# Attention and a gated feed-forward on one core: the value steps and the feed-forward of a batch start one score burst later, and v is normed ahead of the out copies

## The chip, the cores and the metric

The kernel runs on one core of one Trainium2 chip. A core has five engines that each work through their own queue in order: TensorE (PE in the profile) for matrix products, VectorE (DVE), ScalarE (ACT), GpSimd (POOL) and SyncE (SP), which here only issues DMA transfers. They wait for one another by semaphores. TensorE writes its products into PSUM, eight banks of 128 partitions x 2 KB; the other engines read them from there.

The metric is the time of one execution on the device in microseconds (us), as the median of several runs.

## The reference

The input is q (8 batches, 16 heads, 384 rows, 64 columns), k and v (8, 4, 384, 64), and the weights of a feed-forward layer. Each of the four k and v heads serves four q heads.

```python
scores = scale * np.matmul(q, k.transpose(0, 1, 3, 2))
attn = np.exp(scores - max) / sum            # softmax over the keys
x = np.matmul(attn, v)                       # heads side by side: 384 x 1024 per batch
h = np.maximum(x @ w_in, 0.0)                # 384 x 1024
u, v = h[..., :512], h[..., 512:]
v_n = (v - mean(v)) / np.sqrt(var(v) + 1e-06)
v_s = np.einsum('ts,bsd->btd', w_spatial, v_n) + b_spatial[None, :, None]
out = (u * v_s) @ w_out                      # 384 x 1024 per batch
```

## The kernel before

**Steps and a written order.** Every piece of work is a small step with a short name, and the order of the steps is written out by hand as text. `play` (L618) reads the words one after the other and calls the function behind each; the instructions reach each engine's queue in that order. A word without a mark belongs to batch b of the round, one with `'` to batch b-1, with `''` to b-2, with `+` to b+1. A round therefore works on four batches at once: attention scores of b, values and the middle of the feed-forward of b-1, the output product of b-2, loads for b+1.

**The steps**, with the engine that does them:

- `s` (L301): one score tile for two heads, two matmuls of 512 columns that run side by side in the two halves of the array's rows, into a pair of PSUM banks. `e` (L318): ScalarE's exp of that pair into aT, 1.02 us. A batch has 18 of them, s0 to s8 for the first group of heads and s9 to s17 for the second. They are played in bursts of three.
- `a` (L339): VectorE adds two of three key tiles of aT into sT (fp16). Six of them a batch (a00 to a02, a10 to a12).
- `m` (L352): TensorE sums aT over the keys with a matrix of ones. `r` (L359): ScalarE makes 1/sum by Ln and Exp. `x` (L374): values, attn times v. `n` (L387): VectorE multiplies the value tile by 1/sum into xT. The constants `C0` and `C1` (L638, L639) hold the sums, recs, values and norms of the first and of the second group of heads.
- `V` (L431): v half of x @ w_in for one third of the rows, and VectorE's relu from PSUM (L436). `S` (L443): mean and variance (L449, L450). `rs` (L452): ScalarE's 1/sqrt of the variance. `vn` (L457): VectorE norms v, three instructions (L460).
- `p` (L470): spatial product of one 128-column tile, and VectorE's bias add (L480). `U` (L484): u half, and VectorE's relu times v_s into gT (L493).
- `O` (L498): output product of half a row third, VectorE's copy to osb (L513), and after each second one the transfer to memory on the SP queue (L521). `Oc` is the same, done in four column groups of 32; `Oa` is the same with the copy on ScalarE.
- `lk lq lv` (L178 to L210): loads on the SP queue. `ck cq cv`: casts to fp16 on GpSimd (L189, L232, L200). `tk tq` (L249, L255): transposing transfers on the SP queue.

**PSUM banks.** `take1` and `take2` (L87 to L98) give out the bank, or the even pair of banks, that has been unused longest. A step that takes a bank waits for the last reader of what was in it. In a round the last burst behind V2, O2, O3 takes the two banks of V2 and O2, so it waits for VectorE's copy of O2; p0 and U0 take the banks of the values x010 and x011, so they wait for VectorE's norms.

**The round.** The list `VISITS` (L640) has six entries, each a burst of three score tiles and a block of other work. The first rounds (`RAMP`, `RAMP1`, `FIRST`) and the tail (`LAST`) have texts of their own. The loop that plays them stands at L667 to L671. In the steady text TensorE runs around a ring: burst, Oc pair and values of the second heads, burst, V0 V1, burst, V2 O2 O3, burst, Oc pair and values of the first heads, burst, p0 U0 p1 U1, burst, p2 U2 p3 U3, and again.

Of the kernel before, what the change touches and what calls it, by code (L numbers as in the profile page):

```python
# [13 lines left out]
ALU = mybir.AluOpType  # L14
# [3 lines left out]
def kernel(  # L18
# [11 lines left out]
    nc = tc.nc  # L30
# [145 lines left out]
    T = {}  # L176
# [159 lines left out]
                    stop=(t == n - 1),  # L336
                )

    def add(b, gp, c):  # L339
        aT = T["aT", b, gp]  # L340
        if ("sT", b, gp) not in T:
            T["sT", b, gp] = ff.tile([P, 2, G * S], FP16, name=f"sT_{b}_{gp}", tag="part")
        cs = slice(c * 512, (c + 1) * 512)
        nc.vector.tensor_tensor(T["sT", b, gp][:, :, cs], aT[:, 0, :, cs], aT[:, 1, :, cs], ALU.add)  # L344

    def add2(b, gp, c):
        T["all", b, gp] = True
        cs = slice(c * 512, (c + 1) * 512)
        sT = T["sT", b, gp][:, :, cs]
        nc.vector.tensor_tensor(sT, sT, T["aT", b, gp][:, 2, :, cs], ALU.add)  # L350

    def sums(b, gp, quad):  # L352
        x = take_of_pair(("sums", b, gp)) if b else take1()
# [103 lines left out]
    def v_norm(b, engine):  # L457
        for st in range(NST):
            v_n = vp.tile([P, DH], FP16, name=f"v_n_{b}_{st}", tag="v_n")
            engine.tensor_scalar(  # L460
                v_n,
                T["v_r", b, st],
                T["mv", b][:, st, 0:1],
                T["rstd", b][:, st : st + 1],
                op0=ALU.subtract,
                op1=ALU.mult,
            )
            T["v_n", b, st] = v_n
# [88 lines left out]
    def project_last(b, i, parts=2):  # L557
# [20 lines left out]


    STEPS = {  # L580
        "w": idle, "s": score, "e": expo, "m": sums, "a": add, "f": add2, "r": recip, "rd": recip_v, "x": value, "n": norm,
        "V": gate_v, "S": stats, "rs": rstd, "vn": lambda b: v_norm(b, nc.vector),
        "p": spatial, "U": gate_u, "O": project, "A": v_half, "H": u_half,
        "lk": load_k, "lq": load_q, "lv": load_v,
# [33 lines left out]
    def play(b, text):  # L618
        for word in text.split():
            kind = word.rstrip("'+")  # L620
            at = b - word.count("'") + word.count("+")
            op = kind.rstrip("0123456789")
            nums = kind[len(op):]
            if 0 <= at < B:
                STEPS[op](at, *([int(nums)] if op in ("s", "e", "w") else map(int, nums)))
# [12 lines left out]
    C1 = "m10' m11' r10' r11' x100' n100' x101' n101' x110' n110' x111' n111'"  # L638
    C0 = "m00 m01 r00 r01 x000 n000 x001 n001 x010 n010 x011 n011"  # L639
    VISITS = [  # L640
        "s0 s1 s2 e0 e1 e2 a12' Oc0'' Oc1'' lk+ lq0+ lv+ lq1+", C1,
        "s3 s4 s5 e3 e4 e5 V0' S0' V1' S1' a00 a01 ck+ cq0+",
        "s6 s7 s8 e6 e7 e8 V2' S2' O2'' O3'' tk+ tq0+ cq1+ cv+",
        "s9 s10 s11 e9 rs' e10 e11 a02 Oc4'' Oc5'' vn' tq1+", C0,
        "s12 s13 s14 e12 e13 e14 p0' U0' p1' U1' a10",
        "s15 s16 s17 e15 e16 e17 p2' U2' p3' U3' a11",
    ]
    STEADY = " ".join(VISITS)
    FIRST = """lk+ lq0+ lv+ lq1+
        s3 e3 s4 e4 V0' S0' s5 e5 V1' S1' ck+ cq0+  # L650
        s6 e6 s7 e7 V2' S2' s8 e8 Q11 tk+ tq0+ cq1+ cv+
# [1 line left out]
        s12 e12 s13 e13 p0' U0' s14 e14 p1' U1'   # L653
        s15 s16 s17 e15 e16 e17 p2' U2' p3' U3' a10 a11"""
    LAST = """
        a12' Oc0'' Oc1'' m10' m11' r10' r11' x100' n100' x101' n101' x110' n110' x111' n111'
        V0' S0' V1' S1' V2' S2' O2'' O3'' rs' vn' O4'' O5''
        pz0' pz1' pz2' pz3' Uz0' Uz1' O0' O1' Uz2' Oh2' Oh3' Oh4' Oz5'"""

    with tc.manual_schedule():  # L660
        play(0, RAMP)
        nc.vector.memset(warm, 0.0)
        make_identity(nc, ident)
        nc.vector.tensor_copy(ident16, ident)
        nc.vector.memset(ones32, 1.0)
        nc.vector.memset(eps_t, eps_ln)
        play(0, RAMP1)  # L667
        play(1, FIRST)
        for b in range(2, B):
            play(b, STEADY)  # L670
        play(B, LAST)  # L671
# [1 line left out]
_INS = ['q', 'k', 'v', 'moe_w_in', 'moe_w_spatial', 'moe_b_spatial', 'moe_w_out']  # L673
# [26 lines left out]
```

The softmax here doesn't subtract the row's maximum and nothing guards it: scores larger than these inputs give would overflow.

## Time and profile before

| what | us |
|---|---|
| median of 6 runs (256.51 to 259.99) | 257.25 |
| the profiled execution | 256.91 |
| its span, first to last instruction | 255.1 |
| TensorE busy in it | 240.2 |
| VectorE busy | 186.3 |
| ScalarE busy | 172.2 |
| GpSimd busy | 58.6 |
| one steady round, first V0 matmul of batch 5 to that of batch 6 (144.32 to 173.21) | 28.89 |

All times in the text are microseconds from the start of the profiled span, or lengths. The span is what the instructions cover; the execution has some 1.8 us around it. TensorE's granted clock was 0.996 over the span. Because the matmuls overlap, TensorE's time for a step is best read from the start of its first matmul to the start of the next step's.

### The profile page before, as it was taken

Reading aid. Unit: us, or ns where it says so; the run is one execution under the profiler, and the core shown is the slowest. Engines: PE = TensorE matmul, PEld = TensorE weight load, DVE = VectorE, ACT = ScalarE, POOL = GpSimd, SP = SyncE. Lnnn points to the kernel's source line nnn. Section 1 sums busy time; section 2 is a strip of 40 time slices with the busy share of each in tenths; the row PEclk is TensorE's granted clock in tenths of the full one; section 3 lists DMA queues with packets and bytes.
Section 4 is the critical chain, followed back from the end, with each engine's and each line's share of the span. In section 5 each row is a group of like instructions: output and inputs, shape, how many; then the busy total and the mean of one; then the engine's idle time right before and its main releaser. Section 6 shows DMA issues by size and latency. Waiting matters only on the chain.

```text
span 255.1 us, 6119 instructions
## 1 busy us (share of the span) xinstructions
PE 240.2 (94%) x2545; PEld 116.8 (46%) x2545; DVE 186.3 (73%) x348; ACT 172.2 (68%) x228; POOL 58.6 (23%) x100
## 2 busy tenths in 40 slices
PE   6689998999999999999999999999999999999993
PEld 5242434444444535553354434553454534554671
DVE  1534589997977599677977599577986599587953
ACT  3899799877767868677766958776776959730000
POOL 2627922604400064003700063001800000000000
PEclk9999999999999999999999999999999999999998
DMA  6999999959690779529591687519791204010424
GB/s 179 276 250 322 176 175 263 236 136 311 178 217 0 223 231 169 152 83 283 177 221 18 198 256 204 117 45 270 224 216 23 85 0 167 3 72 13 164 84 166
DMA packets 57228, 41.98 MB, mean 165 GB/s; under 512 B 26352, under 2 KB 53360, under 8 KB 57200
## 3 DMA queue, kind: packets, MB, share of 16 engines
q1 hardware_dynamic: 54208, 38.31, 55.8%
q0 software_dynamic: 2848, 3.15, 7.9%
q8 instruction: 20, 0.33, 0.5%
q10 hardware_dynamic: 144, 0.13, 0.1%
q14 instruction: 8, 0.07, 0.1%
HBM read 25.95 MB, written 12.58 MB: 151 GB/s over the span
## 4 chain that ended last, share of the span: by engine, by line
PE 58%; DVE 19%; DMA 11%; POOL 5%; issue 3%; SPq 2%; ACT 0%
PE banks L119 44%; DMA q<-in_q_dram 9%; PE banks L331 7%; PE banks L309 7%; DVE osb L513 3%; DVE sT L344 3%; DVE bn L449 3%; DVE v_n L460 3%; DVE v_r L436 3%; DVE xT L391 3%; DMA qT<-q 2%; POOL w_in L142 2%; POOL q L232 1%; SPq L183 1%; POOL ws L162 1%
## 5 line engine op out<-in xcount | busy, mean ns | idle before, releaser
L321 ACT ACTIVATE aT<-banks 128x1024 f16<-128x1024 f32 x144 | 137.5, 1024 | 48.6 <-PE banks L309 47.7
L309 PE MATMUL banks<-qT,kT 64*128 64x512 f16 x288 | 45.7, 380 | 6.6 <-DVE osb L513 2.0
L119 PE MATMUL banks<-xT,w_in 128*128 128x384 f16 (+1 forms) x320 | 47.2, 294 | 0.6 <-DVE v_r L438 0.6
L119 PE MATMUL banks<-w_out,gT 128*32 128x512 f16 (+2 forms) x508 | 45.4, 378 | 0.0
L119 PE MATMUL banks<-w_in,xT 128*128 128x512 f16 x192 | 44.7, 380 | 0.0
L391 DVE TENSOR_TENSOR xT<-banks,rec 128x384 f16<-128x384 f32 x64 | 31.4, 550 | 10.1 <-ACT rec L364 8.3
L232 POOL CAST q<-q 128x384 f16<-128x384 f32 x56 | 31.9, 602 | 17.2 <-DMA q<-in_q_dram 16.6
L119 PEld LDWEIGHTS <-w_in 128*128 128x128 f16 x320 | 27.2, 98 | 15.9 <-issue 1.4
L331 PE MATMUL banks<-aT,v 128*32 128x384 f16 x768 | 34.4, 326 | 0.0
L513 DVE COPY osb<-banks 128x512 f32<-128x512 f32 x47 | 31.4, 686 | 3.9 <-PE banks L119 3.8
L119 PEld LDWEIGHTS <-gT 128*32 128x32 f16 (+1 forms) x508 | 18.8, 96 | 27.9 <-issue 9.6
L189 POOL CAST k<-k 128x768 f16<-128x768 f32 x7 | 5.8, 830 | 102.3 <-DMA k<-in_k_dram 93.5
L119 PEld LDWEIGHTS <-xT 128*128 128x128 f16 x192 | 17.2, 98 | 25.6 <-issue 7.4
L344 DVE TENSOR_TENSOR sT<-aT 128x1024 f16<-128x1024 f16 x39 | 27.9, 744 | 0.0
L493 DVE SCALAR_TENSOR_TENSOR gT<-banks,vs 128x384 f16<-128x384 f32 x24 | 13.4, 558 | 17.0 <-PE banks L119 17.0
L331 PEld LDWEIGHTS <-v 128*32 128x32 f16 x768 | 20.4, 97 | 11.1 <-issue 0.9
L309 PEld LDWEIGHTS <-kT 64*128 64x128 f16 x288 | 11.3, 94 | 29.2 <-issue 22.8
L436 DVE TENSOR_SCALAR v_r<-banks 128x512 f32<-128x512 f32 x21 | 14.4, 688 | 11.8 <-PE banks L119 11.1
L119 PE MATMUL banks<-wsT,v_n 128*128 128x384 f16 x96 | 20.8, 327 | 0.8
L362 ACT ACTIVATE rec<-banks 128x384 f32<-128x384 f32 x32 | 15.7, 489 | 4.7 <-PE banks L331 4.3
L480 DVE TENSOR_TENSOR vs<-banks,bias_tp 128x384 f32<-128x384 f32 x28 | 15.6, 557 | 2.9 <-PE banks L119 2.9
L364 ACT ACTIVATE rec<-rec 128x384 f32<-128x384 f32 x32 | 16.7, 523 | 1.0
(49 smaller groups left out, 139.2 us busy)
## 6 DMA issues: line engine op xcount, KB each, us to landing
q<-in_q_dram SPq DMA_DIRECT2D x31, 384.0 KB, 7.0
out_dram<-osb SPq DMA_DIRECT2D x22, 512.0 KB, 3.2
v<-in_v_dram SPq DMA_DIRECT2D x8, 384.0 KB, 6.9
k<-in_k_dram SPq DMA_DIRECT2D x7, 384.0 KB, 5.2
w_in<-in_moe_w_in_dram POOLq DMA_DIRECT2D x16, 128.0 KB, 6.7
w_out<-in_moe_w_out_dram POOLq DMA_DIRECT2D x2, 512.0 KB, 8.7
out_dram<-osb SPq DMA_DIRECT2D x3, 256.0 KB, 2.0
ws<-in_moe_w_spatial_dram SPq DMA_DIRECT2D x1, 576.0 KB, 9.8
```

Source lines behind the costliest of these rows:

```text
L119: nc.tensor.matmul(dst[c : c + cols], w[:, c : c + cols], m, start=(i == 0), stop=(i == n - 1))
L232: engine(T["q16", b, gp][:, 2 * qd : 2 * qd + 2, :, half, :], T["q32", b, gp][:, qd, 2 * half : 2 * half + 2, :].rearrange("p j (t d) -> p ...
L309: nc.tensor.matmul(banks[:, xs[half], :], T["kT", b][lo:hi, t, gp, :], rhs[lo:hi, c * 512 : (c + 1) * 512], start=True, stop=True,)
L321: nc.scalar.activation(T["aT", b, gp][:, t, :, c * 512 : (c + 1) * 512], banks[:, x : y + 1 : y - x, :], AF.Exp, scale=scale)
L331: nc.tensor.matmul(dst[32 * i : 32 * (i + 1), :], weights if len(weights.shape) == 2 else weights[:, half, :], a[:, half, j * S : (j + 1) ...
L344: nc.vector.tensor_tensor(T["sT", b, gp][:, :, cs], aT[:, 0, :, cs], aT[:, 1, :, cs], ALU.add)
L362: nc.scalar.activation(rec, f32(x, S), AF.Ln)
L364: nc.scalar.activation(rec, rec, AF.Exp, scale=-1.0)
L391: nc.vector.tensor_tensor(T["xT", b][:, gp * 4 + quad * 2 + jj, :], f32(x, S), T["rec", b, gp, quad], ALU.mult)
L436: nc.vector.tensor_scalar(v_r, banks[:, x, :], 0.0, None, op0=ALU.max)
L480: nc.vector.tensor_tensor(vs, f32(x, S), bias_tp, ALU.add)
L513: copy(osb[:, half * 512 : (half + 1) * 512], banks[:, x, :])
```

## The change

It moves three things in the written order and adapts the ends to it.

First, in the steady text the blocks behind the bursts move on by one: the Oc pair with C1 stands behind s3 to s5 instead of s0 to s2, V0 V1 behind s6 to s8, V2 O2 O3 behind s9 to s11, the second Oc pair with C0 behind s12 to s14, p0 to U1 behind s15 to s17; p2 to U3 move into the next round, behind its s0 to s2. The loads of the next batch stay with the first burst, and so stand ahead of the Oc1 transfer on the SP queue and behind that of Oc5. The adds get one place in each visit: a00 behind Oc1 and a01 behind S1 (both stood behind S1), a10 behind Oc5 and ahead of C0, a11 behind U1.

Second, `rs` stands behind V2 and S2 in the same visit, and `vn` behind O2, O3 and a02, ahead of the copies of Oc4 and Oc5 (it stood behind them).

Third, the ends. Batch 2 gets a text `SECOND`, in which the steps that the first rounds have already done are replaced. In `LAST` p2 to U3 are added, O2's copy moves to ScalarE and `vn` stands ahead of O3, O4 and O5.

`add` and `add2` get an argument for the engine, and two step names use it; no text plays those names.

```diff
     VISITS = [
-        "s0 s1 s2 e0 e1 e2 a12' Oc0'' Oc1'' lk+ lq0+ lv+ lq1+", C1,
-        "s3 s4 s5 e3 e4 e5 V0' S0' V1' S1' a00 a01 ck+ cq0+",
-        "s6 s7 s8 e6 e7 e8 V2' S2' O2'' O3'' tk+ tq0+ cq1+ cv+",
-        "s9 s10 s11 e9 rs' e10 e11 a02 Oc4'' Oc5'' vn' tq1+", C0,
-        "s12 s13 s14 e12 e13 e14 p0' U0' p1' U1' a10",
-        "s15 s16 s17 e15 e16 e17 p2' U2' p3' U3' a11",
+        "s0 s1 s2 e0 e1 e2 a12' p2'' U2'' p3'' U3'' lk+ lq0+ lv+ lq1+",
+        "s3 s4 s5 e3 e4 e5 Oc0'' Oc1'' a00 ck+ cq0+", C1,
+        "s6 s7 s8 e6 e7 e8 V0' S0' V1' S1' a01 tk+ tq0+ cq1+ cv+",
+        "s9 s10 s11 e9 e10 e11 V2' S2' rs' O2'' O3'' a02 vn' tq1+",
+        "s12 s13 s14 e12 e13 e14 Oc4'' Oc5'' a10", C0,
+        "s15 s16 s17 e15 e16 e17 p0' U0' p1' U1' a11",
     ]
     STEADY = " ".join(VISITS)
+    SUBS = "Oc0'' Oc1''=>Oc2'';p2'' U2'' p3'' U3''=>O0'' O1'';O2'' O3''=>O3''"
+    SECOND = STEADY
+    for x in SUBS.split(";"):
+        SECOND = SECOND.replace(*x.split("=>"), 1)
...
     LAST = """
-        a12' Oc0'' Oc1'' m10' m11' r10' r11' x100' n100' x101' n101' x110' n110' x111' n111'
-        V0' S0' V1' S1' V2' S2' O2'' O3'' rs' vn' O4'' O5''
+        a12' p2'' U2'' p3'' U3'' Oc0'' Oc1'' m10' m11' r10' r11' x100' n100' x101' n101' x110' n110' x111' n111'
+        V0' S0' V1' S1' V2' S2' Oa2'' rs' vn' O3'' O4'' O5''
         pz0' pz1' pz2' pz3' Uz0' Uz1' O0' O1' Uz2' Oh2' Oh3' Oh4' Oz5'"""
...
         for b in range(2, B):
-            play(b, STEADY)
+            play(b, STEADY if b > 2 else SECOND)
         play(B, LAST)
```

More of the change, by code (lines that the diff above doesn't have):

```diff
@@ L337, in tiles, with add @@
                 )
-    def add(b, gp, c):
+    def add(b, gp, c, engine=nc.vector):
         aT = T["aT", b, gp]
@@ L343, in add, with add2 @@
         cs = slice(c * 512, (c + 1) * 512)
-        nc.vector.tensor_tensor(T["sT", b, gp][:, :, cs], aT[:, 0, :, cs], aT[:, 1, :, cs], ALU.add)
-    def add2(b, gp, c):
+        engine.tensor_tensor(T["sT", b, gp][:, :, cs], aT[:, 0, :, cs], aT[:, 1, :, cs], ALU.add)
+    def add2(b, gp, c, engine=nc.vector):
         T["all", b, gp] = True
@@ L349, in add2 @@
         sT = T["sT", b, gp][:, :, cs]
-        nc.vector.tensor_tensor(sT, sT, T["aT", b, gp][:, 2, :, cs], ALU.add)
+        engine.tensor_tensor(sT, sT, T["aT", b, gp][:, 2, :, cs], ALU.add)
     def sums(b, gp, quad):
@@ L580 @@
     STEPS = {
-        "w": idle, "s": score, "e": expo, "m": sums, "a": add, "f": add2, "r": recip, "rd": recip_v, "x": value, "n": norm,
+        "w": idle, "s": score, "e": expo, "m": sums, "a": add, "f": add2,
+        "ap": lambda b, gp, c: add(b, gp, c, nc.gpsimd), "fp": lambda b, gp, c: add2(b, gp, c, nc.gpsimd),
+        "r": recip, "rd": recip_v, "x": value, "n": norm,
         "V": gate_v, "S": stats, "rs": rstd, "vn": lambda b: v_norm(b, nc.vector),
```

## The prediction

> **What bounds the kernel now.** I read first the page's busy row and its digits per slice, then the chain of waits inside one steady batch, then the timelines of TensorE, GpSimd and the SP queue, then single groups.
>
> ```profile
> PE 240.2 (94%) x2545; PEld 116.8 (46%) x2545; DVE 186.3 (73%) x348; ACT 172.2 (68%) x228; POOL 58.6 (23%) x100
> ```
>
> TensorE is the bound, so a change of order alone can only win back its waits. The chain between 147 and 160 us (batch 5; start, length, what) shows where they are:
>
> ```profile
> 147.98 0.70 DVE v_r L436
> ...
> 149.62 1.58 DVE sT L344 x2
> 151.20 0.61 DVE v_r L436
> ...
> 152.66 0.68 DVE osb L513
> 153.34 0.04 issue
> 153.39 0.37 PE banks L309
> 153.76 1.87 PE banks L119 x32
> 155.63 0.02 issue
> 155.65 0.69 DVE osb L513
> 156.34 0.47 DVE v_n L460 x2
> ...
> 158.09 1.03 DVE xT L391 x2
> 159.12 0.04 issue
> 159.16 0.97 PE banks L119 x5
> ```
>
> For 11 us VectorE leads: TensorE gets the last bank of a score burst when the O2 copy is done, and p0 gets its bank when the third norm is done. The first wait in TensorE's timeline:
>
> ```profile
> 152.19 0.82 PE L309 MATMUL banks<-qT,kT 64*128 64x512 f16 x5
> 153.39 0.37 PE L309 MATMUL banks<-qT,kT 64*128 64x512 f16 x1 [0.38 <-DVE osb L513]
> ```
>
> The burst lasts 1.50 instead of the 0.75 of every unhindered one; the burst before p0 lasts 1.03 (158.13 to 159.16). So 1.03 of this batch's 28.84 us is waiting. From the first V0 matmul to p0 it takes 14.84 us; without waits 3.56 (V0, V1) + 0.75 + 1.74 (V2) + 1.82 (O2, O3) + 0.75 + 1.74 (Oc4, Oc5) + 0.65 (sums) + 2.05 (values) + 0.75 = 13.81. Batches 2 to 7 take 14.89, 14.74, 15.08, 14.84, 14.79, 14.43 (V0 at 57.45, 86.39, 115.18, 144.32, 173.21, 202.06; p0 at 72.34, 101.13, 130.26, 159.16, 188.00, 216.49). From p0 to the next V0 it is 14.05 each time (159.16 to 173.21), without waits: four bursts, one Oc pair, one value block and two p/U blocks add up to it. All that can be won there is about 5.9.
>
> Why batch 7 is quicker is the second thing to see. It has no casts:
>
> ```profile
> L344 DVE TENSOR_TENSOR sT<-aT x39: 657/684/996, 52.3 to 225.8; 128x1024 f16<-128x1024 f16 x39
> L460 DVE TENSOR_SCALAR v_n<-v_r,mv,rstd x24: 530/541/1048, 41.8 to 238.1; 128x512 f16<-128x512 f32 x24
> 146.47 0.83 POOL L189 CAST k<-k 128x768 f16<-128x768 f32 x1 [19.70 <-DMA k<-in_k_dram]
> 155.04 0.82 POOL L200 CAST v<-v 128x768 f16<-128x768 f32 x1
> 142.19 0.43 SPq L183 DMA_DIRECT2D k<-in_k_dram  x1
> ```
>
> An add alone takes 0.68; those that lie over GpSimd's casts take up to 0.99. The casts run from 146.47 to 155.86, because the loads stand on the SP queue behind the Oc1 out transfer (141.80).
>
> **The cyclic order of TensorE stays.** Burst, Oc pair with values, burst, V0 V1, burst, V2 O2 O3, and so on is the same ring as before; only the burst in front of each block has another number. Going through take1 and take2 with the new text gives the same ring of banks: the last burst behind V2, O2 still takes their two banks, p0 and U0 still take those of n010 and n011. No instruction is added or lost in the steady part. What changes is VectorE's order, the SP queue's and both ends.
>
> **VectorE from V0 to p0, with V0 at 0.** Rows: back to back, a relu, stats and aggregate take 1.55, a copy or add 0.60, a v_n 0.46, a norm 0.465. The V1 relu starts at 3.66 and its stats end at 5.21, as before. a00 is gone from here; a01 ends at 5.87 and costs nothing, because V2's relu can't start before V2 is done: 4.31 + 1.93 (V0 starts at 144.32, its relu at 146.25) = 6.24. Before it started at 6.80 (batch 5) or 6.39 (batch 7). Aggregate done, O2 copy 7.79 to 8.46; its burst, whose last half would go at 8.31, goes at 8.53: a loss of 0.22 where 0.75 was. O3 copy 8.39, a02 8.99, v_n 9.59, Oc4 copy 10.97, Oc5 11.57, a10 12.17, n000 12.77, third norm done at 14.25, p0 at **14.30**. Three edits meet here: v_n ahead of the Oc copies changes no sum, since both stand ahead of the norms, but fills the time in which VectorE waited for Oc4 and Oc5 (0.06 + 0.17 in batch 5, 0.26 + 0.17 in batch 7); a10 now stands ahead of the norms and costs 0.60; a00 gone saves what V2's relu gains. TensorE by itself would want p0 at 13.81, so 0.49 stays lost. ScalarE: the rstd pair waits for the stats (7.95), ends at 8.45 and delays e12 by 0.15; r00 and r01 are done at 12.37 and 13.30, before the norms that read them.
>
> **The queues.** In the new text the six loads stand behind Oc5's transfer, not Oc1's; Oc5's copy ends at 12.26. Their targets are free: all casts of the round before are over. Issued from 12.6 on, with the delays of batch 5 (k cast 4.3 after its issue, v cast ended 13.7 after it), the casts run from 17 to 26.3, that is beside p/U and the Oc1 block, and end 7 us before a01 of the next round (33.5). They now meet a11, a12 and a00. A price of 0.31 each (0.99 - 0.68): a11 and a12 push p2's bias add back by 1.0, but the burst that takes these banks starts 0.9 after the last use ends; a00 ends 4.3 after its burst, and the norms there wait for rec until 4.25 anyway. Cover gone, 0.05 to 0.3 a batch. The transposes issue right behind Oc1's transfer, about 2 us ahead of V0 instead of 10 us after it, and nothing waits for them: the only wait for a qT is batch 2's first burst, which the old text governs. GpSimd's own order is unchanged.
>
> **A rule that speaks against it.** The Trainium skill, "SBUF — State Buffer", section "SBUF: two separate sides": VectorE (two-port modes or two SBUF inputs) and GpSimd share a port pair as an exclusive lock, the loser blocks for a whole instruction. The row agrees in kind: 1048 against 541 for a v_n beside a k cast. Before, v_n begins 0.40 after the last cast (156.26 to 155.86). Moved forward by 2 us and with the casts where they were, three v_n would each be held; by the row 3 x 0.51 = 1.5 a batch, by the rule up to 0.82 (the v cast) more than once. With the casts moved, by both 0. I take 0.
>
> **Batch 2** (the second text) has less TensorE work in front, so ScalarE leads. s0 at 51.50 as before (it waits for qT). O0 O1 end at 53.99; s5 needs e2 (54.78) and loses 0.32; Oc2 at 55.14; values end at 58.72; e5 ends at 57.5, so the recs come late, s8 waits for n101 (0.34) and V0 for n110 (59.97): V0 at 60.02. Then without O2 in the chain p0 is at +13.75 = 73.77.
>
> **Sum.** V0 of batch 3 at 73.77 + 14.05 = 87.82; four periods of 14.30 + 14.05 = 28.35 lead to V0 of batch 7 at 201.22, p0 at 215.52. p0 to U1 3.57 and p2 to U3 3.68 (moved here, with no burst between): Oc0 of the last text at 222.77, before 224.59: **-1.82**. **The end**: v_n started at 237.24, behind two copies; mv is done at 236.14, rstd at 236.70 (rows), so now 236.80. pz lost 0.59 (two gaps of 0.46 against 0.16), now about 0.1; the O2 copy on ScalarE has no row, nearest the 0.49 of 128x384 and 1.02 of 128x1024: 0.5 to 0.7, and it ends by 236.1, before mv. The three copies behind v_n end at 240.0 and the bias adds at 241.9, as late as TensorE's first Uz needs them. **-0.45**, bounds -0.1 to -0.6. Together -2.27: 256.91 (profiled execution; its span is 255.1) becomes 254.6, and on the median of the runs, 257.25, it is **255.0**.
>
> **Rivals.** *Half of it* (0.17): casts still reach into the V0-to-p0 stretch, or a00 and the recs hold V0 back by 0.25 a batch. For it: a00 at its slow price ends within 0.1 of the norms' start. 5 x 0.25 = 1.2 less, 256.2.
>
> *Nothing* (0.08): the VectorE chain has the same members (a00 out, a10 in), stays as long, and the end's gain pays for batch 2's loss: 257. For it: in batch 7, where no cast disturbs, my 14.30 is only 0.13 under the row. Against it: batches 3 to 6 took 0.44 to 0.78 more than that.
>
> *More* (0.08): the norms don't bind and V0 to p0 takes 13.81; 5 x 0.49 + 0.8 more, 251.8 at the extreme. Against it: the sum of VectorE's rows, all measured.
>
> *Slower* (0.07): v_n meets the casts. They must still run 9 us after V0, 11 later than I place them; then a02 and v_n cost 0.3 + 1.5 more, p0 comes at 16.1, 1.3 over today in four batches: 5 for them, about 262 with the rest. It is a loss from 0.5 a batch on. For it: batch 0's 1048 ns row. Against it: nothing ahead of the loads on the SP queue waits that long.
>
> **How the numbers follow.** My case has 0.60 and its own range 254.3 to 255.7. The 1% bound (254.7 and 259.8, about what a measurement of this kernel can tell from no change) cuts it: 0.22 of it and the 0.08 of *more* are faster, 0.30; slower 0.08; the rest same, 0.62. The range 253.8 to 257.3 leaves out *slower* and most of *more*.
>
> **What would show it.** The k cast some 3 us after p0; adds of 0.68 between V0 and p0; a burst behind V2, O2, O3 of 0.95 to 1.0; TensorE then waiting for xT, not for osb; V0 to p0 of 14.3; V0 of batch 2 near 60.0; rstd to v_n without copies between at the end. Wrong if p0 comes over 14.8 after V0, or if V0 waits for norms.

## The result and the profile after

The changed kernel takes 255.18 us in the median of 28 runs (253.73 to 256.64), the kernel before 256.76 in the median of its runs on the same chips (255.56 to 259.99): ratio **0.9936**, 95% interval 0.9922 to 0.995, or 1.6 us less. The forecast was 255.0, a gain of 2.27 on the profiled execution. The profiled execution of the changed kernel took 254.24, its span is 252.5.

Below, "batch n" is the round whose text is played for batch n, as in the prediction; its V0 to p0 steps carry the data of batch n-1.

The chain of waits of the changed kernel around the same stretch (start, length, what; "..." marks lines left out); V0 of this batch starts at 144.21, so 150.46 is 6.25 after it:

```profile
148.59 1.85 PE banks L119 x8
...
150.46 0.70 DVE v_r L436
...
153.20 0.68 DVE sT L344
153.88 1.37 DVE v_n L460 x3
155.26 0.91 DVE osb L513 x2
...
156.37 0.68 DVE sT L344
...
157.44 1.02 DVE xT L391 x2
...
158.50 1.62 PE banks L119 x9
```

The chain has the predicted shape. It now enters VectorE from TensorE at V2's relu and not at V1's; it does not go back to TensorE in the middle, because VectorE no longer waits for Oc4 and Oc5; it ends, as before, at the third norm, behind a10 (156.37). p0 comes 14.29 after V0.

TensorE's timeline shows the two bursts with what is left of their waits:

```profile
152.09 1.03 PE L309 MATMUL banks<-qT,kT 64*128 64x512 f16 x6
153.04 1.91 PE L119 MATMUL banks<-w_out,gT 128*32 128x512 f16 x32
157.49 0.93 PE L309 MATMUL banks<-qT,kT 64*128 64x512 f16 x6
158.50 0.65 PE L119 MATMUL banks<-wsT,v_n 128*128 128x384 f16 x3
```

From start to next start the first burst takes 0.95 (152.09 to 153.04), the second 1.01; an unhindered one 0.75. The list of TensorE's waits (line, releaser: us in total, times, longest) had this line in the kernel before:

```profile
PE banks L309 <- DVE osb L513: 2.0, 5, 0.6
```

The changed kernel's list has no such line. The burst still waits for the copy a little: its last matmul starts 0.21 after its partner (152.74 and 152.53), released by O2's copy; before it was 0.75 (153.39 and 152.63). The list does not count the 0.21, since the partner still runs and TensorE does not idle. p0 is released by the third norm. The two longer waits of a score burst for the norms, 0.5 and 0.2, lie between 16 and 21 us in both traces and are not part of this stretch.

The loads and casts moved as well. The SP queue, then GpSimd, both in the changed kernel; p0 of the batch before comes at 130.16 and V0 of this one at 144.21:

```profile
128.91 0.53 SPq L521 DMA_DIRECT2D out_dram<-osb  x1
129.50 0.42 SPq L183 DMA_DIRECT2D k<-in_k_dram  x1
```

```profile
135.41 0.97 POOL L189 CAST k<-k 128x768 f16<-128x768 f32 x1 [22.18 <-DMA k<-in_k_dram]
142.64 0.82 POOL L200 CAST v<-v 128x768 f16<-128x768 f32 x1
```

The k load follows Oc5's transfer at once, and the last cast ends at 143.46, ahead of V0. No cast is left beside the adds, v_n and norms that follow, in batches 3 to 7. In batch 2, whose loads and casts fall otherwise, the casts still run from 60.14 to 68.19, between V0 (59.59) and p0 (73.35).

| stretch, from the traces | before | after |
|---|---|---|
| batch 2, first score burst to V0 (with other steps in it after the change) | 5.95 | 8.73 |
| batch 2, V0 to p0 | 14.88 | 13.76 |
| batches 3 to 6, V0 to p0 | 14.74, 15.08, 14.84, 14.79 | 14.28, 14.29, 14.29, 14.29 |
| batch 7, V0 to p0 | 14.44 | 14.29 |
| p0 to the next V0 | 14.05 | 14.05, behind batch 2 14.19 |
| V0 of batch 2 to the last V0 | 171.66 | 167.35 |
| last V0 to the end | 26.04 | 25.53 |
| first burst of batch 2 to the end | 203.65 | 201.61 |

From the first burst of batch 2 on, the changed kernel is 2.04 shorter. The spans differ by 2.7 because that first burst began at 51.50 in the one trace and 50.87 in the other. The text up to there is the same in both; the burst waited for a qT transfer in the first and not in the second. This wait differs from execution to execution, see the last section, so the 0.6 is no gain of the change.

### The profile page after: what moved, and what is told of

The parts are those of the page before. It is cut to its first block, busy times and chain, and to the rows that moved or that the text cites. A ratio compares the mean times of both kernels' runs of the same rounds, so it can differ in the third digit from the quotient of the medians.

```text
span 252.5 us, 6100 instructions
## 1 busy us (share of the span) xinstructions
PE 242.2 (96%) x2533; PEld 118.6 (47%) x2533; DVE 183.7 (73%) x347; ACT 172.5 (68%) x229; POOL 55.0 (22%) x100
## 4 chain that ended last, share of the span: by engine, by line
PE 63%; DVE 22%; ACT 6%; issue 5%; DMA 2%; SPq 0%; POOL 0%; DVEq 0%
PE banks L119 47%; PE banks L309 8%; PE banks L331 7%; DVE xT L391 5%; ACT aT L321 4%; DVE osb L513 3%; DVE sT L344 3%; DVE v_n L460 3%; DVE bn L449 2%; DVE v_r L436 2%; DMA q<-in_q_dram 1%; ACT rec L364 1%; DMA out_dram<-osb 1%; DVE v_r L438 1%; ACT rec L362 1%
## 5 line engine op out<-in xcount | busy, mean ns | idle before, releaser
L513 DVE COPY osb<-banks 128x512 f32<-128x512 f32 x46 | 30.3, 684 | 8.9 <-PE banks L119 8.9
L232 POOL CAST q<-q 128x384 f16<-128x384 f32 x56 | 28.9, 549 | 18.6 <-DMA q<-in_q_dram 18.1
L344 DVE TENSOR_TENSOR sT<-aT 128x1024 f16<-128x1024 f16 x39 | 27.6, 724 | 0.0
L449 DVE BATCH_NORM_STATS2 bn<-v_r 128x6 f32<-128x512 f32 x24 | 16.7, 695 | 0.8
```

Of the source, the lines that this page charges most:

```text
L232: engine(T["q16", b, gp][:, 2 * qd : 2 * qd + 2, :, half, :], T["q32", b, gp][:, qd, 2 * half : 2 * half + 2, :].rearrange("p j (t d) -> p ...
L344: engine.tensor_tensor(T["sT", b, gp][:, :, cs], aT[:, 0, :, cs], aT[:, 1, :, cs], ALU.add)
L449: nc.vector.bn_stats(bn, T["v_r", b, st])
L513: copy(osb[:, half * 512 : (half + 1) * 512], banks[:, x, :])
```

## The experiments

Eleven experiments were run, each timed against the kernel before; the last is the changed kernel once more. Theory A is the one of the prediction. Theory B says that the gain came from the casts' new place alone and VectorE's order is free, theory C that only the order counts. "V0 to p0" is that of batches 3 to 7 in the trace.

| kernel | V0 to p0 | median us | ratio to before, interval |
|---|---|---|---|
| before | 14.44 to 15.08 | 256.8 to 257.0 | |
| changed | 14.29 | 255.18 | 0.9936, 0.9922 to 0.995 |
| changed, again, timed together with the last three below | 14.29 | 254.49 | 0.9909, 0.9879 to 0.9939 |
| changed, a10 behind the norms | 14.03 | 253.55 | 0.9856, 0.9812 to 0.99 |
| changed, loads behind Oc1 | 14.30 to 15.32 | 258.2 | 1.0035, 1.001 to 1.006 |
| changed, v_n behind the Oc copies | 14.90 | 258.5 | 1.0046, 1.0025 to 1.0067 |
| changed, O2's copy on ScalarE behind rstd, a10 behind the norms | 14.48 | 255.47 | 0.9944, 0.9925 to 0.9963 |
| before, loads ahead of the Oc pair | 14.44 | 256.13 | 0.9962, 0.9935 to 0.999 |
| changed, end undone | 14.29 | 255.12 | 0.9925, 0.9891 to 0.9959 |
| before, v_n ahead of the Oc copies | 14.17 to 15.16 | 257.09 | 1.0033, 1.0004 to 1.0062 |
| O2's copy on ScalarE ahead of rstd, a10 behind the norms | 13.82 | **251.89** | 0.9802, 0.976 to 0.9843 |
| the same, batch 2's values one burst earlier | 13.82 | 252.84 | 0.9827, 0.9783 to 0.987 |
| changed, a00 back ahead of a01 | 14.43 | 255.74 | 0.9963, 0.9931 to 0.9994 |

**a10 alone.** It undoes one part that the prediction had priced at 0.60 on VectorE's chain.

```diff
-        "s12 s13 s14 e12 e13 e14 Oc4'' Oc5'' a10", C0,
+        "s12 s13 s14 e12 e13 e14 Oc4'' Oc5''", C0, "a10",
```

> The changed kernel with one add moved: a10 stands behind the values and norms of the first heads, no longer ahead of them. Theory A (VectorE's chain from V2's relu to the third norm sets p0): a10 costs its 0.60 us there; without it the norms wait for rec, the third is done 13.88 after V0, and p0 comes when TensorE is ready, 13.81 plus the 0.22 of the O2 copy: 14.03 instead of 14.29. Five batches of 0.26 and some 0.6 in batch 2: 1.9 us less than the changed kernel, about 253.3. Theory B (the gain came from the casts' new place alone, VectorE's order is free): V0 to p0 stays 14.3 and the time 255.2.

V0 to p0 became 14.03 in all five batches and the median 253.55. Theory B falls: one add of 0.68 us that stands behind the norms instead of ahead of them is worth another 0.8% of the kernel's time, with no instruction taken away. In the trace V0 of batch 2 to the last V0 takes 165.91, 1.44 less than in the changed kernel; the 1.9 that were expected are not all there, since V0 to p0 of batch 2 became shorter by 0.06 only and not by 0.6.

**The loads back behind Oc1.** The queue part undone.

```diff
-        "s0 s1 s2 e0 e1 e2 a12' p2'' U2'' p3'' U3'' lk+ lq0+ lv+ lq1+",
-        "s3 s4 s5 e3 e4 e5 Oc0'' Oc1'' a00 ck+ cq0+", C1,
+        "s0 s1 s2 e0 e1 e2 a12' p2'' U2'' p3'' U3''",
+        "s3 s4 s5 e3 e4 e5 Oc0'' Oc1'' a00 lk+ lq0+ lv+ lq1+ ck+ cq0+", C1,
```

> The changed kernel with the six loads of a batch back behind Oc1's transfer on the SP queue. The casts then run from about 2 to 11.5 us after V0, beside a01, a02 and the v_n. Theory A with the shared port: a02 and the three v_n stretch by 0.3 and up to 1.5, p0 comes 14.6 to 16.1 after V0, so 1.5 to 8 us more than the changed kernel in all: 256.7 to 263, no better than the kernel before. Theory B: the gain falls away entirely, 256.8. Theory C (only VectorE's order counts, the casts' place doesn't): V0 to p0 stays 14.3, 255.2.

It is slower than the kernel before, by 0.9 (interval 0.3 to 1.5). VectorE's and GpSimd's timelines of this kernel in batch 5 show why; three v_n take 2.46 where they take 1.45 without casts:

```profile
155.57 2.46 DVE L460 TENSOR_SCALAR v_n<-v_r,mv,rstd 128x512 f16<-128x512 f32 x3
```

```profile
155.64 1.15 POOL L232 CAST q<-q 128x384 f16<-128x384 f32 x2 [1.50 <-DMA q<-in_q_dram]
156.74 1.01 POOL L200 CAST v<-v 128x768 f16<-128x768 f32 x1
```

The v_n and the casts slow each other: a v_n takes 0.72 to 1.04 instead of 0.54, the v cast 1.01 instead of 0.82. V0 to p0 is 14.85 in batch 3, 15.17 to 15.32 in batches 4 to 6, and 14.30 in batch 7, which has no casts. This is the *slower* rival of the prediction, made to happen, below its price (0.6 to 1.0 a batch, not 1.8). Theory C falls.

**v_n back behind the Oc copies.**

```diff
-        ... V2' S2' rs' O2'' O3'' a02 vn' tq1+",
-        "s12 s13 s14 e12 e13 e14 Oc4'' Oc5'' a10", C0,
+        ... V2' S2' rs' O2'' O3'' a02 tq1+",
+        "s12 s13 s14 e12 e13 e14 Oc4'' Oc5'' vn' a10", C0,
```

> The changed kernel with the three v_n back behind the copies of Oc4 and Oc5, all else as changed. Theory A: VectorE then waits for Oc4 (0.34) and Oc5 (0.26), a10 and the norms come 0.60 later, p0 at 14.9 after V0: 3.6 us more in six batches, about 258.8, slower than the kernel before. Theory B: no difference, 255.2.

V0 to p0 is 14.90 in batches 3 to 7, as worked out, and the median 258.5. With the casts in their new place and a10 ahead of the norms, the new place of v_n is what keeps the change from being a loss. VectorE's timeline of this kernel shows the waits that it fills: 0.26 for Oc4 and 0.17 for Oc5 (L513), and from there v_n, a10 (157.81) and the norms (158.41) follow without a gap.

```profile
154.97 0.69 DVE L513 COPY osb<-banks 128x512 f32<-128x512 f32 x1 [0.26 <-PE banks L119]
155.84 0.69 DVE L513 COPY osb<-banks 128x512 f32<-128x512 f32 x1 [0.17 <-PE banks L119]
156.44 1.45 DVE L460 TENSOR_SCALAR v_n<-v_r,mv,rstd 128x512 f16<-128x512 f32 x3
```

**O2's copy on ScalarE, behind rstd.** An attempt to shorten the chain further.

```diff
-        "s9 s10 s11 e9 e10 e11 V2' S2' rs' O2'' O3'' a02 vn' tq1+",
-        "s12 s13 s14 e12 e13 e14 Oc4'' Oc5'' a10", C0,
+        "s9 s10 s11 e9 e10 e11 V2' S2' rs' Oa2'' O3'' a02 vn' tq1+",
+        "s12 s13 s14 e12 e13 e14 Oc4'' Oc5''", C0, "a10",
...
```

Here and in the next kernel the list `SUBS` is adapted to the new word, so that batch 2 still leaves the step out.

> The changed kernel with a10 behind the norms and the steady O2 copy on ScalarE (behind the rstd pair). Theory A: the burst behind V2, O2, O3 no longer waits for VectorE (0.75 instead of 0.97), the norms wait only for ScalarE's rec, p0 comes 13.9 to 14.0 after V0: 2.0 to 2.6 us less than the changed kernel, about 252.8. If ScalarE becomes the bound instead (the copy behind rstd delays e12 to e14 by 0.6, the recs and so the third norm by as much), p0 comes at 14.4 and the time is 255.5 to 256. Theory B: 255.2.

The second case came: 14.48, 255.47. ScalarE's timeline in batch 5 of this kernel, then the burst's last matmul in TensorE's:

```profile
153.97 0.30 ACT L454 ACTIVATE rstd<-mv,eps_t 128x3 f32<-128x3 f32 x1 [1.08 <-DVE mv L450]
154.30 0.20 ACT L455 ACTIVATE rstd<-rstd 128x3 f32<-128x3 f32 x1
154.41 0.57 ACT L513 COPY osb<-banks 128x512 f32<-128x512 f32 x1
```

```profile
155.03 0.37 PE L309 MATMUL banks<-qT,kT 64*128 64x512 f16 x1 [0.29 <-ACT osb L513]
```

The copy stood behind a step that waits for the stats: ScalarE idles for 1.08, then come rstd and the copy, and the burst waits for the copy.

**The same copy ahead of rstd.** The edit is against the kernel just shown.

```diff
-        "s9 s10 s11 e9 e10 e11 V2' S2' rs' Oa2'' O3'' a02 vn' tq1+",
+        "s9 s10 s11 e9 e10 e11 V2' S2' Oa2'' rs' O3'' a02 vn' tq1+",
```

> The changed kernel with a10 behind the norms and O2's copy on ScalarE ahead of the rstd pair (in the run with it behind the pair, the copy waited for the stats and held e12). Theory A: the copy lies in ScalarE's idle time, 7.1 to 7.7 after V0, e12 starts at 8.45 as in the changed kernel, the burst behind O3 takes 0.75, the norms wait for rec, p0 comes 13.9 after V0 (14.03 with a10 moved alone, 13.81 is TensorE's own): 0.5 to 0.8 us below the run with a10 alone, about 253.0. If ScalarE is late anyway: 14.1 or more and no gain over that run.

```profile
150.33 0.59 ACT L513 COPY osb<-banks 128x512 f32<-128x512 f32 x1 [0.27 <-PE banks L119]
151.14 0.30 ACT L454 ACTIVATE rstd<-mv,eps_t 128x3 f32<-128x3 f32 x1 [0.22 <-DVE mv L450]
```

The copy now lies in time that ScalarE had free. V0 to p0 is 13.82: TensorE's own work without a wait (13.81 in the prediction). It is the fastest kernel of the study, with a median of 251.89, below the kernel before and the changed one: the round takes 27.88 where it took 28.35 in the changed kernel and 28.9 before.

**One part alone on the kernel before: the loads.**

```diff
-        "s0 s1 s2 e0 e1 e2 a12' Oc0'' Oc1'' lk+ lq0+ lv+ lq1+", C1,
+        "s0 s1 s2 e0 e1 e2 a12' lk+ lq0+ lv+ lq1+ Oc0'' Oc1''", C1,
```

> The kernel before with one part of the change alone: the six loads ahead of the Oc pair in the first visit, so that on the SP queue they no longer wait for Oc1's copy. The casts then end before V0. Theory A: all batches look like batch 7 of the kernel before, 14.43 from V0 to p0, with adds of 0.68: 1.8 us less than before, about 255.0. Theory B (this is the whole gain): the same 255.2 as the changed kernel. Theory C (order only): no difference to before, 256.8.

V0 to p0 is 14.44 in batches 3 to 7, so each of them now looks like the one that has no casts. From V0 of batch 2 on the trace is 1.71 shorter than before (169.96 + 26.03 against 171.66 + 26.04). The timed gain is 1.0 (interval 0.3 to 1.7), less than the 1.8 expected; the profiled execution lost 1.7 in batch 2's first blocks to a lower clock, told below, and whether others did so too stays open. Theory C falls here too. The casts' new place alone thus gives most of what the whole change gives (1.71 of 2.04 in the traces, 1.0 of 1.6 in the timings).

**One part alone on the kernel before: v_n ahead of the Oc copies.**

```diff
-        "s9 s10 s11 e9 rs' e10 e11 a02 Oc4'' Oc5'' vn' tq1+", C0,
+        "s9 s10 s11 e9 rs' e10 e11 a02 vn' Oc4'' Oc5'' tq1+", C0,
```

> The kernel before with one part of the change alone: v_n ahead of the copies of Oc4 and Oc5, with the casts where they were. v_n then falls on the casts of q and v. By the row (a v_n of 1.05 beside a cast): up to 0.5 more on two or three of them, less the 0.23 of filled waiting: 0.3 to 1.2 later p0 in four batches, 1 to 5 us slower than before, 258 to 262. If the casts don't hold v_n, the filled waits alone count: 0.2 to 0.4 in six batches, 255 to 255.6.

Neither of the two expected cases came. The ratio says 0.8 slower (interval 0.1 to 1.6), the medians differ by 0.1 (257.09 and 257.02), and in the trace V0 of batch 2 to the last V0 is 0.3 shorter than before: a change of time is not shown. In batches 2 and 7 the stretch is 0.25 and 0.27 shorter, which is the filled waiting; in 3 to 6 v_n takes 0.72 to 1.04 beside the casts, and the stretch is 14.82 to 15.16, as long as before. The two effects about cancel. Alone, the loads bring the batches with casts to 14.44 and v_n ahead leaves them at 14.82 or more; v_n ahead needs the casts out of the way.

**a00 back.**

```diff
-        "s3 s4 s5 e3 e4 e5 Oc0'' Oc1'' a00 ck+ cq0+", C1,
-        "s6 s7 s8 e6 e7 e8 V0' S0' V1' S1' a01 tk+ tq0+ cq1+ cv+",
+        "s3 s4 s5 e3 e4 e5 Oc0'' Oc1'' ck+ cq0+", C1,
+        "s6 s7 s8 e6 e7 e8 V0' S0' V1' S1' a00 a01 tk+ tq0+ cq1+ cv+",
```

> The changed kernel with a00 back behind S1, ahead of a01. Theory A: the two adds end at 6.41 after V0, 0.17 after V2 is ready, so everything behind comes 0.17 later: p0 14.46 instead of 14.29, 0.9 to 1.0 us more in six batches, about 256.1. Rival (VectorE has slack there, the burst or rec decides): 14.29 and 255.2.

V0 to p0 is 14.43, by 0.14 more than in the changed kernel and not by the 0.60 of an add: V2's relu starts 6.40 after V0, with a00 gone 6.25, and no earlier because V2 is not done. The medians of the two on one chip (255.74 and 254.49) are in that order, with overlapping intervals.

**The end undone.**

```diff
-        V0' S0' V1' S1' V2' S2' Oa2'' rs' vn' O3'' O4'' O5''
+        V0' S0' V1' S1' V2' S2' O2'' O3'' rs' vn' O4'' O5''
```

> The changed kernel with the end undone: O2's copy on VectorE, and v_n behind the copies of O2 and O3. Theory A: the three v_n start 0.45 later, the spatial products wait, the kernel takes 0.45 us more than the changed one, 255.6; the steady part is untouched (14.29 from V0 to p0). Rival: the end is bound by TensorE's products anyway, 255.2.

In the trace the last V0 to the end takes 26.04 again, against 25.53, with V0 to p0 unchanged in batches 3 to 7: the end is worth 0.51. The timing can't resolve it (0.9925, 0.9891 to 0.9959, against 0.9936).

**Batch 2's values earlier**, on top of the fastest kernel: the sums and values of the second heads go ahead of s3 in `SECOND`.

```diff
         SECOND = SECOND.replace(*x.split("=>"), 1)
+    SECOND = SECOND.replace(C1 + " ", "", 1).replace("lk+ lq0+ lv+ lq1+", "lk+ lq0+ lv+ lq1+ " + C1, 1)
```

> The kernel with a10 behind the norms and O2's copy on ScalarE ahead of rstd, and in batch 2 the sums and values of the second heads one burst earlier, behind O0 and O1. Theory A: batch 2's loss at its start is ScalarE's (six exps ahead of the recs that the norms need, which hold the banks of s8 and V0); with the values first, V0 of batch 2 comes 0.4 to 0.6 earlier after its first burst than the 8.7 of the changed kernel, and all else stays: 252.5. Rival: the exps of two bursts then pile up behind the recs and hold the third burst instead: 8.7 or more, 253.0 or more.

The rival holds: first burst to V0 took 8.99, not 8.55 as in the fastest kernel. The second burst is unhindered, but the third takes 1.96, since the exps of two bursts now follow one another with only Oc2 between. TensorE waits in it twice for an exp, for 0.33 and then:

```profile
60.14 0.39 PE L309 MATMUL banks<-qT,kT 64*128 64x512 f16 x2 [0.52 <-ACT aT L321]
```

In both orders that were run, ScalarE sets what batch 2 costs at its start.

**The changed kernel again.**

> The changed kernel itself once more, beside the others on one chip. Theory A: 14.29 from V0 to p0 in batches 3 to 7, and about 1.6 to 2.0 us below the kernel before; if its profile's 2.6 us were the true gain, 2.6.

The trace repeats (8.69, 167.38 and 25.53 against 8.73, 167.35 and 25.53). The ratio of 0.9909 makes the gain 2.3, interval 1.6 to 3.1; it agrees with the 2.0 of the traces and doesn't exclude the 2.7 between the two profiled executions.

## Why the prediction was right

- **The chain from V0 to p0.** Predicted 14.30, measured 14.28 to 14.29 in five batches. The parts hold one by one: a01 hidden behind V2 (relu at 6.24 predicted, 6.25 measured), a10 on the chain (0.26 back when it is moved), v_n worth 0.61 through the waiting that it fills (14.90 without it), the burst behind O3 at 0.95 for a predicted 0.22 over 0.75. (The 28.84 that the prediction gives for the round of batch 5 is a slip; V0 to V0 it is 28.89.)
- **The queues.** The k cast was placed at 17 and the last one's end at 26.3 after the V0 before; measured 19.5 and 27.6 (135.41 and 143.46 less 115.87). That is 1 to 2.5 late, but still out of the stretch in batches 3 to 6, which was what counted. About 1 of it came on the SP queue itself: the issue of a transposing transfer held it for 3.39 until 128.82, so that the loads left at 129.50, 13.6 after V0 and not from 12.6 on. The *slower* rival was real and was kept off by the SP queue alone.
- **The rule on the shared port.** It was taken at 0 since the casts move; with the casts moved back it costs 0.6 to 1.0 a batch, between the nothing and the 1.8 of the rival. The longest of those v_n, 1.04, lie over the v cast: they are 0.50 over their own 0.54, and the cast, at 1.01, is 0.19 over its own 0.82. Both got longer, and neither by the whole length of the other. The runs show the conflict; they do not show that one of the two blocks for a whole instruction.
- **Batch 2** was mis-sized at its start. The prediction had 8.52 from first burst to V0 (60.02 less 51.50); measured 8.73 and 8.69. ScalarE leads as worked out, shown by the chain of the changed kernel there:

```profile
54.22 2.85 ACT aT L321 x3
57.08 0.39 ACT rec L362
57.49 0.53 ACT rec L364
```

  The difference is in the first output block: it took 2.17 instead of 1.83, because TensorE waited for gT of batch 0, when the first burst came early and had no wait of its own; where the burst came later (the fastest kernel, 51.15) there is no such wait and the stretch is 8.55. And one a00 beside the v cast took 1.32, over the 0.99 that was the largest row before:

```profile
84.77 1.32 DVE L344 TENSOR_TENSOR sT<-aT 128x1024 f16<-128x1024 f16 x1
```

  So V0 of batch 3 came 0.14 late, inside the 0.05 to 0.3 given for the lost cover. Together this is some 0.3 of the 2.27. From V0 to p0 batch 2 took 13.76 for a predicted 13.75, and this closeness is partly luck: the working had no cast there, but a02 lay over the v cast and took 0.78. In the kernel with the end undone, whose text is the same up to the last round, a02 took 1.09 and p0 came 14.08 after V0.
- **The end**: -0.45 predicted, -0.51 in the traces and in the kernel with the end undone.
- **The sum**: -2.27 predicted, -2.04 in the traces from batch 2 on, -1.6 (1.3 to 2.0) and -2.3 (1.6 to 3.1) in the two timings. Between the traces and the first timing 0.4 stays unexplained; it is smaller than what one wait at the start differs by. That the first median fell so near the forecast (255.18 for 255.0) owes something to the starting value, which was 257.25 from six runs and is 256.76 from 63.
- **Rivals.** *Half of it* named a00 as a danger, and a00 did cost 0.14, once. *More* (13.81) was not reached by this change, but by moving a10 and one copy on top of it: the norms did bind.

## What to carry to other kernels

In a kernel whose busiest engine is nearly full, an order is worth what it does to the chain of the second engine: list its instructions between the point where the first engine feeds it and the point where the first engine waits for it, and everything that nobody behind that point needs (here a10) belongs behind it. A step moved on one engine can be worth a gain or a loss by what a third engine does at that moment, so look up what its DMA queue will start earlier or later. Ahead of an instruction that waits, put the work that is ready.

## What the runs showed of the hardware

**The wait at the start differs from run to run.** The text up to the first burst of batch 2 is the same in all thirteen traces, yet that burst starts between 50.29 and 52.67. TensorE does not idle ahead of it in the five traces in which qT is there in time, and idles for 0.54 to 2.16 in the other eight. The transposing transfer of qT is not what differs most: from the start of its issue to its landing it took 5.47 where the burst came first (50.29) and 4.50 in the run with the longest wait, but its issue began at 44.04 in the one and at 47.83 in the other, behind loads and casts that came later. Why they came later is open. So one trace against one other can be off by over 2 us, more than this change is worth.

**A lower clock after such a wait.** In the run of the kernel before with the loads ahead, TensorE waited 2.16 for qT:

```profile
52.46 0.82 PE L309 MATMUL banks<-qT,kT 64*128 64x512 f16 x6 [2.16 <-DMA qT<-q]
```

From 53.58 to 56.99, a stretch of 3.41 that began 1.1 after the matmuls had started again, its granted clock was 0.50, and matmuls of 512 columns in the Oc pair started 427 ns apart instead of 216; after that the clock was 1.00. The Oc pair took 3.06 instead of 1.74. Waits of 1.46 and 1.57 at the same place (the run with O2's copy behind rstd, the run with a00 back) were followed by no such drop. That the wait caused the drop is likely, but with one case not shown.

**In a conflict either instruction can get longer, or both.** In the kernel with the loads back behind Oc1, a v_n over a q cast took 0.72 instead of 0.54 and the q cast 0.69 instead of 0.51. In the kernel before, an add that began just ahead of a q cast (182.64 and 182.65) took its usual 0.68 and the cast 1.04, and an add that began inside one (179.01, the cast from 178.60) took 0.99. So the cost of an overlap has to be looked up on both engines.
